# Opening of a fused attention and gated linear unit kernel: load queues, tail layout, weight order and roots

## The chip, the cores and the metric

The kernel runs on one core of one Trainium2 chip. The metric is device time in microseconds (us), the median of several runs. The core's engines are TensorE (PE; its weight loads are listed as PEld), VectorE (DVE), ScalarE (ACT), GpSimd (POOL) and SyncE (SP). SP computes nothing here and issues most of the transfers (DMAs). A "q" after an engine's name in the profile means its sequencer, which issues DMAs and waits.

## The reference

```python
def _attn_ref(q, k, v, g_norm):            # q, k, v: (8, 8, 576, 64): batch, head, token, width
    kv = np.einsum('bhsd,bhse->bhde', k, v)
    out = np.einsum('bhsd,bhde->bhse', q, kv)
    rms = np.sqrt(np.mean(out * out, axis=-1, keepdims=True) + 1e-06)
    return (out / rms * g_norm).astype(np.float32)

def _moe_ref(x, w_val, conv_w, w_out):     # x: (8, 576, 512), the heads side by side
    xp = np.concatenate([np.zeros((B, K - 1, D), dtype=np.float32), x], axis=1)
    for k in range(K):                     # K = 5
        gate_pre += conv_w[k][None, None, :] * xp[:, k:k + S, :]
    gate = 1.0 / (1.0 + np.exp(-gate_pre))
    val = x @ w_val
    return (gate * val @ w_out).astype(np.float32)
```

q, k and v are divided into 8 batches that don't depend on each other. The weights w_val, conv_w and w_out come in 64 bits and are narrowed to 32 on the chip.

## The kernel before

**An order written out by hand.** The kernel is a set of small functions, called steps, and a string PLAN of some 1,100 calls such as `raw_product 0 3`. The steps are issued in exactly that order, so each engine gets its instructions in the order in which the plan names the steps. An engine works through its own list in order; between engines, waits are set where data require them. A place in PLAN is thus a place in the lists of all engines that the step uses, and in the DMA queue.

**One batch.** `load_half` (L297 for batch 0, L301 for others) brings 512 tokens of k or v in two halves of heads, `load_tails` (L307) the remaining 64. `kv_product` (L438) makes k transposed times v for all heads, `kv_copy` (L453) moves it from PSUM to `kv_bd`. q is turned so that its width lies on the partitions: in batch 0 by matmuls with the identity (`load_q_rows` L326, `turn_q_rows` L480, `sort_q` L487), in other batches by a transposing load and DVE (`load_q` L317, `turn_q` L464). `raw_product` (L498) gives q times kv for a chunk `c` of 128 tokens (chunk 4 has 64). Then `square` (L512, ACT), `sums` (L524, DVE), the inverse root, and `normalise` (L559 on DVE in batch 0, L555 on ACT after). `turn_x` (L570, PE) with `keep_x` (L577, ACT), or `turn_blocks` with `move_blocks` later on, put x with its channels on the partitions; `halo` (L598, POOL) copies the tokens that the convolution needs from the chunk before. `gate_start`, `gate_tap` (L608, DVE) and `gate_end` make the gate, `val_product` (L620) or `val_fast` (L670) x times w_val, `gated` their product, and `out_product` (L701) or `fast_product` the result.

**Roots.** `powers` (L530) raises the sums to the power -1/2 on POOL. In batch 0 the chunks 4, 1 and 0 (`NEWTON`) go another way: `roots` (L538 to L546) makes them together on DVE by a bit trick and three Newton steps.

**Weights.** `stage_weight` (L341) loads a 64-bit piece: `cw` is conv_w, `wval` and `wout` have four pieces each. `narrow_weight key i n` (n from 0 to 7) makes 32 bits of it: steps 1, 2 and 3 on ACT (L366 to L370), the others on DVE (L361, L373 to L387). The last step of a wval piece multiplies by `gcol`, the column of g_norm. `turn_cw` (L409, PE) turns the narrowed conv weights, `keep_cw` (L414 to L416, DVE) scales them and gcol.

**Fillers.** `keep_warm n` (L427) issues n matmuls of the identity with itself, each of them two records in the profile, into a spare part of the PSUM tile of kv. Nobody reads the result. Since the part lies in the tile that `kv_copy` reads, a filler after a `kv_copy` waits for it.

**Queues.** All loads and stores are issued by SP, save gcol and cw (ACT), `move_blocks` (POOL) and half of the last stores (ACT). Batch 1's k and v are loaded into the tiles vsum and wsum, which are free at that time; the profile names them so.

Of the kernel before, what the change touches and what calls it, by code (L numbers as in the profile page):

```python
# [15 lines left out]
P = 128  # L16
# [3 lines left out]
stage_weight cw 0; load_q_rows 0 0; load_q_rows 0 1; load_half k 0 0; load_half v 0 0; load_tails 0;  # L20
narrow_weight cw 0 0; narrow_weight cw 0 1; narrow_weight cw 0 2; load_half k 0 1; load_half v 0 1;
stage_weight wval 0; keep_warm 5; turn_q_rows 0 0; stage_weight wval 1; turn_q_rows 0 1; stage_weight wval 2;
sort_q 0 0; stage_weight wval 3; narrow_weight cw 0 3; turn_q_rows 0 2; sort_q 0 1; narrow_weight cw 0 4;
load_half k 1 0; narrow_weight cw 0 5; narrow_weight cw 0 6; turn_q_rows 0 3; load_half v 1 0; sort_q 0 2;
narrow_weight cw 0 7; load_tails 1; turn_cw; sort_q 0 3; turn_q_rows 0 4; kv_product 0 0; sort_q 0 4;
load_half k 1 1; load_half v 1 1; load_q 1 0; keep_warm 7; kv_product 0 1; load_q 1 1; kv_copy 0; keep_warm 4;
raw_product 0 3; load_q 1 2; raw_product 0 2; square 0 3; raw_product 0 4; sums 0 3; square 0 2;
raw_product 0 1; narrow_weight wval 0 0; square 0 4; powers 0 3; sums 0 2; narrow_weight wval 0 1;
raw_product 0 0; keep_cw; square 0 1; sums 0 4; narrow_weight wval 3 0; powers 0 2; square 0 0; normalise 0 3;
narrow_weight wval 3 1; sums 0 0; keep_warm 5; turn_x 0 3; sums 0 1; keep_x 0 3; normalise 0 2; roots 0;  # L30
keep_warm 5; turn_x 0 2; keep_x 0 2; narrow_weight wval 0 2; normalise 0 4; normalise 0 1; keep_warm 5;
turn_x 0 4; normalise 0 0; keep_x 0 4; narrow_weight wval 0 3; keep_warm 3; turn_x 0 1; halo 0;
narrow_weight wval 0 4; keep_x 0 1; keep_warm 1; kv_product 1 0; narrow_weight wval 0 5;
narrow_weight wval 3 2; narrow_weight wval 0 6; narrow_weight wval 3 3; turn_x 0 0; narrow_weight wval 0 7;
kv_product 1 1; keep_x 0 0; turn_q 1 0; narrow_weight wval 3 4; load_q 1 3; val_product 0 0 1;
narrow_weight wval 3 5; narrow_weight wval 1 0; narrow_weight wval 3 6; narrow_weight wval 1 1;
narrow_weight wval 3 7; val_product 0 0 0; narrow_weight wval 1 2; stage_weight wout 0; turn_q 1 1;
narrow_weight wval 1 3; narrow_weight wval 2 0; gate_start 0 0; load_q 2 0; narrow_weight wval 1 4;
keep_val 0 0 1; narrow_weight wval 1 5; gate_start 0 2; turn_q 1 2; gate_start 0 1; gate_tap 0 0 3;
load_half k 2 0; kv_copy 1; load_half k 2 1; turn_q 1 3; narrow_weight wval 2 1; load_tails 2;  # L40
narrow_weight wval 2 2; narrow_weight wval 1 6; keep_warm 15; raw_product 1 3; narrow_weight wval 2 3;
narrow_weight wval 1 7; raw_product 1 2; load_half v 2 1; gate_tap 0 2 3; square 1 3; load_half v 2 0;
val_product 0 1 1; sums 1 3; load_q 2 1; narrow_weight wout 0 0; powers 1 3; narrow_weight wval 2 4;
narrow_weight wout 0 1; narrow_weight wval 2 5; keep_val 0 0 0; val_product 0 1 0; narrow_weight wval 2 6;
square 1 2; load_q 2 2; narrow_weight wval 2 7; normalise 1 3; sums 1 2; gate_tap 0 0 2; powers 1 2;
narrow_weight wout 0 2; keep_warm 3; raw_product 1 1; turn_q 2 0; keep_val 0 1 0; gate_tap 0 1 3; turn_x 1 3;
load_q 2 3; square 1 1; val_product 0 2 1; narrow_weight wout 0 3; sums 1 1; keep_x 1 3;
narrow_weight wout 0 4; powers 1 1; normalise 1 2; gate_tap 0 1 2; val_product 0 2 0; stage_weight wout 2;
gate_tap 0 0 1; stage_weight wout 3; gate_tap 0 2 2; normalise 1 1; gate_tap 0 1 1; raw_product 1 0;
narrow_weight wout 0 5; turn_x 1 2; gate_tap 0 0 0; square 1 0; tail_and_kv 1; keep_val 0 2 1; sums 1 0;  # L50
keep_val 0 1 1; keep_val 0 2 0; narrow_weight wout 0 6; keep_x 1 2; powers 1 0; narrow_weight wout 0 7;
gate_end 0 0; turn_q 2 1; turn_x 1 1; square 1 4; load_half k 3 0; gate_tap 0 2 1; kv_copy 2;
val_product 0 3 1; load_q 3 0; sums 1 4; keep_x 1 1; val_sums 0; powers 1 4; normalise 1 0; gated 0 0;
val_product 0 3 0; turn_q 2 2; load_half k 3 1; normalise 1 4; turn_q 2 3; load_half v 3 0; load_half v 3 1;
gate_start 0 3; narrow_weight wout 2 0; turn_x 1 0; gate_tap 0 1 0; load_tails 3; raw_product 2 3; keep_x 1 0;
gate_tap 0 3 3; narrow_weight wout 2 1; turn_x 1 4; raw_product 2 2; gate_tap 0 3 2; stage_weight wout 1;
keep_x 1 4; square 2 3; load_q 3 1; narrow_weight wout 3 0; val_product 1 0 1; keep_val 0 3 1; sums 2 3;
narrow_weight wout 2 2; gate_tap 0 3 1; square 2 2; powers 2 3; narrow_weight wout 2 3; gate_tap 0 2 0;
val_product 1 0 0; load_q 3 2; gate_end 0 1; gate_tap 0 3 0; keep_val 1 0 1; sums 2 2; gate_end 0 2; gated 0 1;
normalise 2 3; val_product 1 1 1; powers 2 2; val_sums 1; narrow_weight wout 2 4; keep_val 0 3 0; halo 1;  # L60
gated 0 2; narrow_weight wout 3 1; raw_product 2 1; gate_end 0 3; turn_blocks 2 3; val_product 1 1 0;
square 2 1; gated 0 3; keep_val 1 0 0; narrow_weight wout 3 2; sums 2 1; normalise 2 2; narrow_weight wout 2 5;
val_product 1 2 1; powers 2 1; turn_q 3 0; narrow_weight wout 2 6; load_q 3 3; gate_start 1 0;
narrow_weight wout 2 7; raw_product 2 0; narrow_weight wout 3 3; gate_tap 1 0 3; normalise 2 1;
val_product 1 2 0; narrow_weight wout 3 4; turn_blocks 2 2; narrow_weight wout 1 0; square 2 0;
narrow_weight wout 3 5; tail_and_kv 2; narrow_weight wout 1 1; sums 2 0; narrow_weight wout 1 2;
gate_tap 1 0 2; powers 2 0; keep_val 1 1 1; turn_q 3 1; narrow_weight wout 1 3; keep_val 1 1 0;
turn_blocks 2 1; val_product 1 3 1; square 2 4; load_half k 4 0; narrow_weight wout 1 4; kv_copy 3; load_q 4 0;
sums 2 4; normalise 2 0; narrow_weight wout 1 5; powers 2 4; turn_q 3 2; val_product 1 3 0;
narrow_weight wout 3 6; normalise 2 4; turn_q 3 3; load_q 4 1; gate_start 1 1; narrow_weight wout 1 6;  # L70
turn_x 2 4; raw_product 3 3; narrow_weight wout 3 7; keep_val 1 2 1; keep_x 2 4; narrow_weight wout 1 7;
raw_product 3 2; load_tails 4; square 3 3; turn_blocks 2 0; out_product 0 1; gate_tap 1 0 1; square 3 2;
move_blocks 2 3; keep_val 1 3 1; load_half v 4 0; sums 3 3; gate_start 1 2; load_half v 4 1; gate_tap 1 0 0;
keep_val 1 3 0; load_half k 4 1; keep_val 1 2 0; val_sums 2; gate_end 1 0; powers 3 3; sums 3 2;
out_product 0 3; gate_tap 1 1 3; gate_tap 1 1 2; powers 3 2; normalise 3 3; gate_tap 1 2 3; turn_q 4 0;
gate_tap 1 1 1; move_blocks 2 2; load_q 4 3; raw_product 3 1; gate_tap 1 1 0; out_product 0 2; square 3 1;
gated 1 0; gate_tap 1 2 2; load_tails 5; gate_start 1 3; sums 3 1; gate_end 1 1; gate_tap 1 3 3; keep_out 0 1;
powers 3 1; keep_out 0 3; gate_tap 1 2 1; out_product 0 0; normalise 3 2; store 0 3; turn_blocks 3 3;
gate_tap 1 2 0; move_blocks 2 1; gate_tap 1 3 2; normalise 3 1; store 0 1; gate_tap 1 3 1; gate_tap 1 3 0;
raw_product 3 0; halo 2; gate_end 1 2; gated 1 1; tail_and_kv 3; gate_end 1 3; load_q 4 2; gated 1 2;  # L80
gated 1 3; val_sums 3; out_product 0 5; square 3 4; square 3 0; sums 3 4; keep_out 0 2; sums 3 0; powers 3 4;
store 0 2; turn_q 4 1; powers 3 0; turn_blocks 3 2; turn_blocks 3 1; out_product 0 4; normalise 3 4;
move_blocks 2 0; turn_q 4 2; keep_out 0 5; turn_q 4 3; keep_out 0 0; store 0 5; normalise 3 0; turn_x 3 4;
kv_copy 4; load_half v 5 0; out_product 0 6; turn_blocks 3 0; load_q 5 0; keep_x 3 4; keep_out 0 4;
move_blocks 3 3; x_sums 2 0; gate_start 2 2; store 0 0; x_sums 2 2; raw_product 4 3; keep_out 0 6;
gate_tap 2 2 3; raw_product 4 2; square 4 3; x_sums 2 1; load_q 5 2; val_fast 2 0 0; sums 4 3; square 4 2;
gate_tap 2 2 2; val_fast 2 0 1; powers 4 3; val_keep 2 0 0; sums 4 2; load_half k 5 1; val_fast 2 0 2;
# [752 lines left out]
```

## Time and profile before

| | us |
|---|---|
| median of 6 runs | 330.39 (329.96 to 331.51) |
| the profiled execution, its own time | 331.51 |
| its span, first to last instruction | 329.7 |
| PE, idle time before L480 for q's loads | 2.9 |
| PE, idle time before L427 for kv_copy | 1.9 |
| PE, idle time before L438 for batch 1's v | 1.4 |
| POOL, L530, 37 roots, mean of one | 1.818 |
| DMA from issue to landing, POOL's xT<-y, median | 3.6 |

The busy time is what an engine's instructions cover; a matmul's end is modelled, so that a busy PE isn't PE at its peak. Idle time of an engine that isn't the bottleneck costs nothing. DMA queue q1 (SP's) moved 49.50 MB, q0 (POOL's) 6.30 MB and q10 (ACT's) 0.28 MB.

### The profile page before, as it was taken

The numbers are of one execution on the slowest core, as the hardware profiler recorded it, in microseconds if no ns is written. First come the engines' busy times: TensorE is split into PE (matmuls) and PEld (weight loads), VectorE is DVE, ScalarE is ACT, GpSimd is POOL, SyncE is SP. The second block draws the span as 40 slices with busy tenths as digits, with TensorE's granted clock in tenths as the row PEclk, the third lists the DMA queues.
The fourth block names the chain that finished last, engine by engine and source line by source line (L and its number), as shares of the span: only waits on it lengthen the run. The fifth ranks groups of instructions, "written<-read, shape, count | busy, mean of one in ns | idle before, by whom it ended". The sixth has DMA issues, their size and how long they took to land.

```text
span 329.7 us, 6026 instructions
## 1 busy us (share of the span) xinstructions
PE 316.1 (96%) x2019; PEld 226.1 (69%) x2019; DVE 249.9 (76%) x445; ACT 190.4 (58%) x530; POOL 136.7 (41%) x175
## 2 busy tenths in 40 slices
PE   4988889999999999999999999999999999999993
PEld 4987788888855668667676847766744773888652
DVE  1139969999999767998799699945988629889611
ACT  2446659999858556568646845656655423534320
POOL 3023015445398639734764486235956700000000
PEclk9999999999999999999999999999999999999999
DMA  6999699899599699779979767021515420120323
GB/s 218 305 319 246 194 292 287 258 283 242 159 241 265 181 250 284 171 202 252 233 168 240 233 176 184 0 58 41 145 27 126 119 64 20 47 64 3 95 64 95
DMA packets 43965, 56.47 MB, mean 171 GB/s; under 512 B 14986, under 2 KB 33438, under 8 KB 43934
## 3 DMA queue, kind: packets, MB, share of 16 engines
q1 hardware_dynamic: 40480, 49.50, 56.5%
q0 software_dynamic: 3072, 6.30, 7.5%
q10 hardware_dynamic: 382, 0.28, 0.4%
q8 instruction: 16, 0.26, 0.4%
q14 instruction: 15, 0.12, 0.1%
HBM read 40.33 MB, written 9.44 MB: 151 GB/s over the span
## 4 chain that ended last, share of the span: by engine, by line
PE 85%; DMA 7%; SPq 3%; ACT 2%; DVE 1%; issue 0%; ACTq 0%
PE out L701 25%; PE va L670 14%; PE raw L498 9%; PE val L620 8%; PE vc L670 7%; PE out L708 4%; PE kv L438 4%; PE a L765 4%; PE vb L670 4%; DMA wsum<-in_v_dram 3%; PE cb L765 3%; DMA gcol<-in_g_norm_dram 2%; DMA vl<-in_v_dram 2%; SPq L301 1%; PE kv L427 1%; SPq L307 1%
## 5 line engine op out<-in xcount | busy, mean ns | idle before, releaser
L530 POOL TENSOR_TENSOR rt<-ss,mhalf 128x8 f32<-128x8 f32 (+1 forms) x37 | 67.2, 1818 | 103.3 <-DVE ss L524 100.6
L608 DVE SCALAR_TENSOR_TENSOR gate<-xT,cwT,gate 128x576 f32<-128x576 f32 x128 | 101.0, 812 | 7.4 <-ACT gate L602 6.2
L701 PE MATMUL out<-wout,gv 128*128 128x512 f32 x192 | 85.8, 594 | 0.0
L701 PEld LDWEIGHTS out<-wout,gv 128*128 128x128 f32 x192 | 35.7, 190 | 38.5 <-issue 35.8
L591 POOL DMA_DIRECT2D xT<-y x96 | 53.0, 558 | 16.2 <-issue 4.8
L555 ACT ACTIVATE x<-raw,rt 128x64 f32<-128x64 f32 x252 | 55.1, 344 | 5.8 <-POOL rt L530 3.1
L498 PEld LDWEIGHTS raw<-kvbd,qT 128*128 128x128 f32 (+1 forms) x320 | 35.7, 180 | 7.3 <-issue 4.2
L524 DVE TENSOR_REDUCE ss<-sq 128x8 f32<-128x520 f32 (+1 forms) x37 | 23.5, 636 | 21.8 <-ACT sq L512 21.5
L498 PE MATMUL raw<-kvbd,qT 128*128 128x128 f32 (+1 forms) x320 | 38.1, 277 | 0.0
L615 ACT ACTIVATE gate<-gate 128x576 f32<-128x576 f32 x32 | 22.1, 696 | 19.1 <-DVE gate L608 19.0
L620 PE MATMUL val<-xT,wval 128*128 128x288 f32 x128 | 32.6, 408 | 0.0
L512 ACT ACTIVATE sq<-raw 128x512 f32<-128x512 f32 (+1 forms) x40 | 22.3, 562 | 17.8 <-PE raw L498 17.6
L620 PEld LDWEIGHTS val<-xT,wval 128*128 128x128 f32 x128 | 23.7, 190 | 6.0
L670 PE MATMUL va<-xs,vsum 128*128 128x288 f32 x96 | 27.2, 406 | 0.0
L716 ACT COPY ot<-out 128x512 f32<-128x512 f32 x28 | 16.1, 586 | 18.4 <-PE out L701 13.2
L633 DVE TENSOR_TENSOR gv<-gv,gate 128x576 f32<-128x576 f32 x32 | 23.4, 754 | 3.8 <-ACT gv L691 2.2
L602 ACT ACTIVATE gate<-xT,cwT 128x576 f32<-128x576 f32 x32 | 24.8, 790 | 0.5 <-DVE gv L633 0.5
L670 PEld LDWEIGHTS va<-xs,vsum 128*128 128x128 f32 x96 | 18.2, 190 | 4.8
L583 DVE STREAM_TRANSPOSE y<-x 128x512 f32<-128x512 f32 x24 | 16.7, 698 | 2.8 <-ACT x L555 2.8
L427 PE MATMUL kv<-ident 128*128 128x128 f32 x106 | 15.0, 293 | 3.3 <-ACT kvbd L453 1.9
L466 DVE STREAM_TRANSPOSE qT<-qs 128x512 f32<-128x512 f32 x24 | 16.7, 696 | 0.7 <-DMA qs<-in_q_dram 0.7
L438 PE MATMUL kv<-v,k 128*64 128x64 f32 x448 | 16.9, 222 | 0.0
(117 smaller groups left out, 438.4 us busy)
## 6 DMA issues: line engine op xcount, KB each, us to landing
qs<-in_q_dram SPq DMA_DIRECT2D x112, 140.0 KB, 4.5
out_dram<-ot SPq DMA_DIRECT2D x140, 64.0 KB, 1.7
k<-in_k_dram SPq DMA_DIRECT2D x12, 512.0 KB, 5.5
v<-in_v_dram SPq DMA_DIRECT2D x12, 512.0 KB, 7.5
xT<-y POOLq DMA_DIRECT2D x96, 64.0 KB, 3.6
y<-in_moe_w_val_dram SPq DMA_DIRECT2D x4, 512.0 KB, 9.0
w_wout<-in_moe_w_out_dram SPq DMA_DIRECT2D x4, 512.0 KB, 4.3
qs<-in_q_dram SPq DMA_DIRECT2D x2, 576.0 KB, 5.0
```

Of the source, the lines that this page charges most:

```text
L438: nc.tensor.matmul(kvp[r * D:(r + 1) * D, hp, :], kl[:, head(hp, r), :] if j == NJ else st["k", b, at[0]][:, at[1], at[2], j, :], vl[:, he ...
L498: nc.tensor.matmul(raw[row * m:(row + 1) * m, col * P:(col + 1) * P], st["qT", b][:, hp, c * P:c * P + m], kv_bd[b % 2][:, hp, :], start=T ...
L524: nc.vector.reduce_sum(out=ss[:, 0:n], in_=st["sq", b, c][:, 0:n], axis=AX.X)
L530: nc.gpsimd.tensor_tensor(out=rt[:, 0:n], in0=st["ss", b, c][:, 0:n], in1=mhalf[:, 0:n], op=ALU.pow)
L555: nc.scalar.activation(out=x[:, to * D:(to + 1) * D], in_=st["raw", b, c][:, h * D:(h + 1) * D], func=AF.Copy, scale=st["rt", b, c][:, h:h ...
L591: nc.gpsimd.dma_start(out=xTs[b % 2][i * TB:(i + 1) * TB, :, first:first + P], in_=y[a * TB:(a + 1) * TB, i])
L602: nc.scalar.activation(out=gate[:], in_=xTs[b % 2][:, jt, HALO:SX], func=AF.Copy, scale=cwT[:, K - 1, jt:jt + 1])
L608: nc.vector.scalar_tensor_tensor(out=gate[:], in0=xTs[b % 2][:, jt, tap * TB:tap * TB + S], scalar=cwT[:, tap, jt:jt + 1], in1=gate[:], op ...
L620: nc.tensor.matmul(val[:], wval[:, kc, jt * P:(jt + 1) * P], xTs[b % 2][:, kc, HALO + n * SV:HALO + (n + 1) * SV], start=(kc == 0), stop=( ...
L633: nc.vector.tensor_tensor(out=both, in0=both, in1=st["gate", b, jt][:], op=ALU.mult)
L670: nc.tensor.matmul(st[bank, "val", b, mj][:], weights_[:, k], tokens()[:, k], start=(n in (0, 1, 3) and k == 0), stop=(k == NK // 2 - 1), ...
L701: nc.tensor.matmul(po[:], gv[:, jt, first:first + P], wout[:, jt, :], start=(jt == 0), stop=(jt == NK - 1),)
```

## The change

It has five parts, and a new PLAN.

1. In batch 0, k's and v's first halves are issued by ACT, the second halves still by SP. The first wval piece is issued by ACT. gcol and cw are issued by POOL, gcol as part of `stage_weight cw`. The first plan steps are now k's half, cw, q's first rows, v's half, q's other rows, tails, wval 0. wval's pieces 2 and 3 are loaded after batch 1's k and v and three of its q loads.
2. The tails of heads 0 to 3 go to partitions 0 to 63 and those of heads 4 to 7 to partitions 64 to 127, in two DMAs each for k and v in place of one. The cleared part of a tail tile is two memsets of half the width in place of one.
3. The activation that loads ACT's table is a step of its own, `warm_up`, after the load of wval 0.
4. `roots` and `NEWTON` are gone: all five chunks of batch 0 use `powers`.
5. In PLAN, 26 fillers and `turn_cw` stand ahead of q's transposes; wval 0 and 1 are narrowed first, their first steps before the raw products; three value products instead of two come before batch 1's raw products, and 6 fillers in place of 15. There are 64 fillers instead of 53. The rest of PLAN holds the same steps in another order.

```diff
-stage_weight cw 0; load_q_rows 0 0; load_q_rows 0 1; load_half k 0 0; load_half v 0 0; load_tails 0;
-narrow_weight cw 0 0; narrow_weight cw 0 1; narrow_weight cw 0 2; load_half k 0 1; load_half v 0 1;
-stage_weight wval 0; keep_warm 5; turn_q_rows 0 0; stage_weight wval 1; turn_q_rows 0 1; stage_weight wval 2;
-sort_q 0 0; stage_weight wval 3; narrow_weight cw 0 3; turn_q_rows 0 2; sort_q 0 1; narrow_weight cw 0 4;
...
+load_half k 0 0; stage_weight cw 0; load_q_rows 0 0; load_half v 0 0; load_q_rows 0 1; load_tails 0;
+stage_weight wval 0; warm_up; load_half k 0 1; load_half v 0 1; stage_weight wval 1; narrow_weight cw 0 0;
+load_half k 1 0; narrow_weight cw 0 1; narrow_weight cw 0 2; load_half v 1 0; narrow_weight cw 0 3;
+load_tails 1; narrow_weight cw 0 4; narrow_weight cw 0 5; narrow_weight cw 0 6; narrow_weight cw 0 7;
+keep_warm 26; turn_cw; load_half k 1 1; load_half v 1 1; load_q 1 0; keep_warm 5; turn_q_rows 0 0;
+turn_q_rows 0 1; sort_q 0 0; turn_q_rows 0 2; sort_q 0 1; kv_product 0 0; narrow_weight wval 0 0; keep_cw;
+turn_q_rows 0 3; narrow_weight wval 0 1; sort_q 0 2; turn_q_rows 0 4; narrow_weight wval 0 2; load_q 1 1;
+sort_q 0 3; keep_warm 4; kv_product 0 1; sort_q 0 4; load_q 1 2; kv_copy 0; narrow_weight wval 1 0;
+narrow_weight wval 0 3; keep_warm 4; raw_product 0 3; narrow_weight wval 1 1; raw_product 0 2; square 0 3;
+stage_weight wval 2; stage_weight wval 3; raw_product 0 4; sums 0 3; square 0 2; raw_product 0 1; square 0 4;
...
+narrow_weight wval 0 7; kv_product 1 1; keep_x 0 1; normalise 0 0; turn_q 1 1; turn_x 0 0; val_product 0 0 1;
+narrow_weight wval 1 6; stage_weight wout 0; keep_x 0 0; narrow_weight wval 1 7; gate_start 0 1; turn_q 1 2;
+gate_start 0 2; val_product 0 1 1; load_q 2 1; narrow_weight wval 2 0; gate_tap 0 2 3; narrow_weight wval 2 1;
+gate_tap 0 1 3; narrow_weight wval 2 2; val_product 0 0 0; gate_tap 0 1 2; gate_start 0 0; load_q 2 0;
+gate_tap 0 2 2; narrow_weight wval 2 3; kv_copy 1; narrow_weight wval 3 0; turn_q 1 3; narrow_weight wval 3 1;
+load_half k 2 0; narrow_weight wval 2 4; keep_val 0 0 1; keep_warm 6; raw_product 1 3; narrow_weight wval 3 2;
...
-                nc.gpsimd.memset(t[T:P], 0.0)
+                nc.gpsimd.memset(t[T:P, 0:HP], 0.0)
+                nc.gpsimd.memset(t[0:T, HP:H], 0.0)
...
-        for r in range(P // D):
-            nc.scalar.dma_start(out=gcol[r * D:(r + 1) * D, :], in_=g_norm.unsqueeze(1))
+
+    def warm_up():
+
         nc.scalar.activation(out=warm[:], in_=warm[:], func=AF.Sigmoid)
...
-                nc.sync.dma_start(
+                (nc.sync if i else nc.scalar).dma_start(
                     out=t[:, r].rearrange("p h j d -> p h (j d)"),
...
-            nc.sync.dma_start(
-                out=tails[b % 2][n][0:T], in_=src[b, :, SF:S, :].rearrange("h s d -> s h d"))
+            for r in range(2):
+                nc.sync.dma_start(
+                    out=tails[b % 2][n][r * T:(r + 1) * T, r * HP:(r + 1) * HP],
+                    in_=src[b, r * HP:(r + 1) * HP, SF:S, :].rearrange("h s d -> s h d"))
...
-        (nc.scalar if key[0] == "cw" else nc.sync).dma_start(
+        (nc.gpsimd if key[0] == "cw" else nc.scalar if key == ("wval", 0) else nc.sync).dma_start(
...
     def stage_weight(*key):
+        if key[0] == "cw":
+            for r in range(P // D):
+                nc.gpsimd.dma_start(out=gcol[r * D:(r + 1) * D, :], in_=g_norm.unsqueeze(1))
         stage(key, *weights[key][0:3])
...
-    def roots(b):
```

## The prediction, made before the changed kernel ran

> **What bounds the kernel now.** First the page's head and busy time by stretch (columns: stretch, length, busy time and instructions of PE, PEld, DVE, ACT, POOL, granted clock, DMA share, GB/s).
>
> ```profile
> span 329.7 us, 6026 instructions
> PE 316.1 (96%) x2019; PEld 226.1 (69%) x2019; DVE 249.9 (76%) x445; ACT 190.4 (58%) x530; POOL 136.7 (41%) x175
> ```
>
> ```profile
> 0.00:10.00 10.00, 5.78 (x36) 5.09 (x38) 1.50 (x18) 2.88 (x6) 2.61 (x10) 1.00 0.75 237
> ...
> 30.00:40.00 10.00, 8.22 (x110) 7.04 (x111) 8.98 (x17) 6.35 (x11) 1.44 (x4) 1.00 0.73 195
> 40.00:50.00 10.00, 8.91 (x63) 7.78 (x62) 7.01 (x13) 6.46 (x13) 1.74 (x1) 1.00 1.06 286
> 50.00:60.00 10.00, 10.00 (x89) 8.68 (x89) 9.89 (x17) 9.35 (x35) 4.16 (x4) 1.00 1.03 288
> ...
> 300.00:330.00 30.00, 24.70 (x103) 16.87 (x101) 11.70 (x23) 6.86 (x15) 0.00 (x0) 1.00 0.28 71
> ```
>
> From 43 us to about 325 PE is never seen idle. So the end is the moment at which PE becomes gapless, plus a fixed amount of PE work. Time can be won or lost in the opening, or by breaking the gapless stretch. Next, PE's waits and its timeline in the opening.
>
> ```profile
> PE qTps L480 <- DMA qs<-in_q_dram: 2.9, 2, 2.1
> PE kv L427 <- ACT kvbd L453: 1.9, 2, 1.1
> PE kv L438 <- DMA wsum<-in_v_dram: 1.4, 1, 1.4
> ```
>
> ```profile
> 1.36 2.50 PE L427 MATMUL kv<-ident 128*128 128x128 f32 x10 [1.36 <-POOL ident masks.py:199]
> ...
> 7.40 6.13 PE L480 MATMUL qTps<-ident,qs 128*64 128x128 f32 x62 [2.12 <-DMA qs<-in_q_dram]
> ...
> 20.36 4.53 PE L498 MATMUL raw<-kvbd,qT 128*128 128x128 f32 x40
> ...
> 37.08 4.15 PE L620 MATMUL val<-xT,wval 128*128 128x288 f32 x16
> 42.31 3.62 PE L427 MATMUL kv<-ident 128*128 128x128 f32 x30 [1.09 <-ACT kvbd L453]
> 45.77 1.95 PE L498 MATMUL raw<-kvbd,qT 128*128 128x128 f32 x16
> ```
>
> Four landmarks: q transposes start at 7.40, batch 0's raw products at R = 20.36, the first value product at V = 37.08, batch 1's raw products at 45.77. Filler (L427) costs 0.25 us a record at the start (2.50/10) and 0.121 later (3.62/30): PE is slow first. Last, the loads.
>
> ```profile
> SPq L297 <- DMA gcol<-in_g_norm_dram: 2.5, 1, 2.5
> ```
>
> ```profile
> 22.79 11.04 DMA wsum<-in_v_dram
> ```
>
> ```profile
> 22.93 3.54 POOL L530 TENSOR_TENSOR rt<-ss,mhalf 128x8 f32<-128x8 f32 x2 [19.66 <-DVE ss L524]
> ...
> 91.14 2.35 POOL L591 DMA_DIRECT2D xT<-y  x4 [4.30 <-DVE gate L608]
> ```
>
> Batch 1's last v half lands at 33.83 and PE stands for it. A load on SP waits for the landing of gcol, a load eight places earlier in the program; later ones do the same: about eight are in flight at a time[...]. The POOL lines price a root (1.77) and a DMA issue (0.59).
>
> [...]
>
> **The change part by part.**
>
> *Start of the q transposes.* It takes from two sides. Data: bytes before batch 0's second q row load grow from 1,152 KB to at most 2,176 KB (first k and v halves come beside it on ACT's queue). At the 237 GB/s of the first stretch, started near 2 us, that is 11.4 at the latest against 7.4. Conv weights: the plan now puts turn_cw and five fillers ahead of the transposes, and gcol and cw are issued by POOL behind eight tail memsets. A 64x512 memset lasts 0.52; half as wide I take 0.3, so POOL is free at 1.36 + 8 x 0.3 = 3.8; three issues at 0.59: 5.5. From start of issue to landing the page shows 3.6 us (median) for POOL's transfers; the small ACT loads of the opening took 5.4 to 6.2. Bounds for cw's landing: 4.9 + 3.6 = 8.5 and 4.9 + 5.4 = 10.3. Narrowing it is five DVE operations and three ACT ones in a row: 0.21 + 3 x 0.43 + 1.04 and gaps, 2.7 us. Then turn_cw (0.2) and five fillers (10 x 0.121 = 1.2). The transposes start at 12.6 to 14.4; I take 13.1. The 26 fillers ahead end before it: roughly 20 records slow, 32 fast, 9 to 10.5 us. A new wait stands on ACT: wval 0 is the eleventh load, so its issue waits for the third, the first q row load, at about 7. Behind it on ACT are the table load (1.28) and cw's three narrowing steps; they are wanted from 8.7 on, so this is covered by cw's own transfer, and costs a us at most if q comes at 8.
>
> *To the raw products.* By then PE runs at full clock. The last 8 transposes took 0.49, so 72 take 4.4 instead of the 6.9 from 7.40 to 14.3. Beside them: two kv products (1.26 each), four fillers (1.0), kv_copy and its wait with four fillers (1.9): R = 13.1 + 4.4 + 2.5 + 1.0 + 1.9 = 22.9, say 22.8. That is 2.4 late. Before kv 0 1 all of batch 0 plus wval 0 must be in: about 3,970 KB, at 250 to 270 GB/s 17 to 18.5 us; PE comes at 20.
>
> *To the first value product.* The eleven small Newton operations on DVE go (27.36 to 29.66, 2.3 us). Five roots now run one behind the other on POOL: from R + 2.6, four at 1.77 and the short one at 1.2, to R + 10.9. DVE, in its new order, fills the time: after two sums, wval 0's and 1's steps, normalisations, the first turn_q. Adding its rows (reduce 0.69, narrow 0.42, 0.68, 0.42, 0.68, 0.75, normalise 0.68, transpose 0.77) behind each root I get the last normalisation done at R + 12.7, its transpose and V at R + 13.3 = 36.1; before it was R + 16.7. This holds only if kv 1 is not late. wval 2 and 3, 1,024 KB, now come after batch 1's k and v: 6,784 KB instead of 7,808 KB are ahead. Scaled from 33.83 with a 2 us start: 2 + 31.8 x 6784/7808 = 29.6, with PE there at 32. Covered by 2 us; if uncovered, V moves with it. Gain at V: 1.0.
>
> *To batch 1's raw products.* Before, 45.77 - 37.08 = 8.7 us held two value products (1.94 each), a 1.09 wait and 15 fillers. The new plan has three and 6 fillers: 5.8, then a wait for kv_copy 1. On ACT one keep_x, three gate_starts (0.76), three narrow steps (0.72) and the copy (0.74) stand in front: V + 6.6. So V + 6.7 + 1.4 = V + 8.1: 0.6 less, and one value product, 1.94, is already paid. Later fillers grow from 3 to 5: 2 x 0.242 = 0.5 back.
>
> *Middle and end.* DVE work up to the last output weight falls by the Newton steps (2.3), two taps (1.5) and what is done before R (1.5), against one sum more (0.6); it starts 2 us later. DVE then keeps some 2 us of lead over PE: nothing lost. tails are twice as many DMAs (some 0.6 us of SP each) on an SP that later waits 69 us for output tiles: nothing. Fillers and the warm activation in the opening lie in waiting time.
>
> Sum: 1.0 + 0.6 + 1.9 - 0.5 = 3.0 us. The profiled run's own time was 331.51 around a span of 329.7; its counterpart would be 328.5 with a span of 326.7. The median of the runs, 330.39, is the measure: **327.4 us**.
>
> **Rivals.** B, roots in a row eat it: the 1.77 us roots and a late q for turn_q 1 0 (its wait was 0.59 before) push V to 37.5; the moved value product still counts. 330.39 - (-0.4 + 0.6 + 1.4) = 328.8. For it: DVE takes its work strictly in order, so one late q load delays the last root's user. Against: those loads have 1 MB less in front.
> C, the middle absorbs it: from 50 to 90 us DVE is 9.8 to 10 and ACT 9.0 to 9.8 of 10 busy; PE would wait and arrive as before, 330.4. Against: PE showed no wait there, and DVE's list got shorter.
> D, slower, the late conv weights: turn_cw stands in PE's order ahead of everything[...]. Each us of lateness past 13.1 goes into R and V, so gain ends at a start of 16.1, cw landing at 12. There PE has also been idle since about 10[...], and the clock can fall: 72 transposes at the slow 6.9 instead of 4.4. With both, start 16.6: -3.5 - 2.5 + 3.0, that is 333.4. Against: the same load took 5.4 us through ACT.
>
> **Numbers.** A, the forecast, 0.45; B 0.11; C 0.09; D with every other loss 0.35. The likeliest's own range is 326 to 329 (start of transposes +-0.9, ACT's chain +-0.7). Over all, 325.8 to 333.2. A difference of 0.2% (0.7 us) is what these runs can tell from none. Faster: A and B, 0.56; same: C, 0.09; slower: D, 0.35.
>
> **What would show it.** Right: q transposes start near 13 and pace at 0.061 us a record; raw near 22.8; first value product near 36 with no wait on v; 6 fillers after three value products, raw of batch 1 near 44; gapless to the end; POOL showing five roots in a row. Wrong: a PE wait of over 3 us at turn_cw with slow transposes behind it (D), DVE standing for qs at turn_q (B), or PE gaps after 50 us (C).

## The result, and the profile after

The changed kernel is slower by 0.45%: 332.5 us in the median of 17 runs (331.08 to 333.8), beside 330.85 (329.96 to 332.45) for the kernel before. The ratio is 1.0045, with a 95% interval of 1.0034 to 1.0057. The forecast was 327.4. The time lies inside the range that was given, but the change went the other way. The ratios here and below leave out a run over 1.5% slower than the fastest of its kernel, of which the experiments have two (331.8 and 334.71 us).

First the head of the page of the changed kernel: span, the PE line, and the clock that PE was granted, in 40 slices of some 8.3 us.

```profile
span 331.1 us, 6118 instructions
PE 318.8 (96%) x2041; PEld 229.4 (69%) x2041; DVE 247.2 (75%) x434; ACT 189.6 (57%) x530; POOL 143.3 (43%) x185
PEclk9879999999999999999999999999999999999999
```

The span grew by 1.4 us, and PE is busy 2.7 us longer. The digits 8 and 7 in the clock line say that the clock fell in slices 2 and 3. (The record of the clock begins with its first rise, here at 6.49 us. Ahead of that the page counts full clock, although the first fillers ran slowly: their 52 records took 8.51 us, where 0.121 each would be 6.3.) The busy time by stretch shows where (columns as in the prediction). From 10 to 20 us it was, in the kernel before,

```profile
10.00:20.00 10.00, 9.16 (x150) 8.63 (x147) 0.97 (x4) 3.14 (x7) 0.00 (x0) 1.00 1.11 317
```

and in the changed kernel

```profile
10.00:20.00 10.00, 5.33 (x37) 5.06 (x39) 2.41 (x10) 1.78 (x4) 0.00 (x0) 0.67 1.13 317
...
40.00:50.00 10.00, 10.00 (x67) 8.37 (x62) 9.00 (x16) 7.99 (x15) 0.10 (x1) 1.00 0.89 244
50.00:60.00 10.00, 10.00 (x52) 8.12 (x52) 9.56 (x17) 7.91 (x28) 6.30 (x3) 1.00 1.11 279
```

From 40 to 60 us PE has no gap, where before it had one in the first half of that (8.91). The loss is in the stretch from 10 to 20: PE is busy for 5.33 us in place of 9.16, at 0.67 of its clock. The DMA engines are as full as before and move the same 317 GB/s. PE's waits name the cause: the list is headed by one wait for the narrowed conv weights, which before cost nothing.

```profile
PE cwps L412 <- DVE cw L387: 4.8, 1, 4.8
...
PE kv L430 <- ACT kvbd L456: 0.9, 1, 0.9
PE kv L441 <- DMA qs<-in_q_dram: 0.6, 1, 0.6
```

The three waits of before are gone (2.9 for q, 1.4 for v) or halved (1.9 for kv_copy); together they were 6.2 us. PE's timeline in the opening:

```profile
1.36 8.51 PE L430 MATMUL kv<-ident 128*128 128x128 f32 x52 [1.36 <-POOL ident masks.py:199]
14.67 0.29 PE L412 MATMUL cwps<-ident,cw 20*128 20x20 f32 x1 [4.81 <-DVE cw L387]
14.89 2.50 PE L430 MATMUL kv<-ident 128*128 128x128 f32 x10
17.32 4.20 PE L483 MATMUL qTps<-ident,qs 128*64 128x128 f32 x48
...
28.26 4.53 PE L501 MATMUL raw<-kvbd,qT 128*128 128x128 f32 x40
...
40.70 5.99 PE L605 MATMUL val<-xT,wval 128*128 128x288 f32 x24
46.61 1.60 PE L430 MATMUL kv<-ident 128*128 128x128 f32 x12
48.05 1.95 PE L501 MATMUL raw<-kvbd,qT 128*128 128x128 f32 x16
```

The fillers end at 9.87. PE stands until 14.67, and the five fillers and the first three groups of q transposes behind the wait run slowly: 0.25 us a filler record (2.50 / 10), as at the start of the kernel, against 0.121 later. The q rows themselves had landed at 6.87. The four landmarks before and after:

| | before | predicted | after |
|---|---|---|---|
| q transposes start | 7.40 | 13.1 | 17.32 |
| batch 0's raw products, R | 20.36 | 22.8 | 28.26 |
| first value product, V | 37.08 | 36.1 | 40.70 |
| batch 1's raw products | 45.77 | 44.2 | 48.05 |
| span | 329.7 | 326.7 | 331.1 |

R is 7.9 us later than before, and 5.6 of that is won back up to batch 1's raw products. What holds the conv weights up is read in the chain of work that ended last (start, length, what):

```profile
3.81 0.30 POOL vl L264
4.11 1.18 POOL gcol L404 x2
5.29 6.71 DMA w_cw<-in_moe_conv_w_dram
...
12.03 0.23 DVE wexp_cw L361
```

The whole beginning of this chain is one small load. POOL clears the tails (eight memsets, 2.75 us from 1.36 to 4.11), issues gcol twice and then the conv weights. Those 20 KB take 6.71 us to land, and narrowing them until 14.63 is the rest of the wait.

### The profile page after: what moved, and what is told of

It is laid out like the page before. It is cut to its first block, busy times and chain, and to the rows that moved or that the text cites. A ratio compares the mean times of both kernels' runs of the same rounds, so it can differ in the third digit from the quotient of the medians.

```text
span 331.1 us, 6118 instructions
## 1 busy us (share of the span) xinstructions
PE 318.8 (96%) x2041; PEld 229.4 (69%) x2041; DVE 247.2 (75%) x434; ACT 189.6 (57%) x530; POOL 143.3 (43%) x185
## 4 chain that ended last, share of the span: by engine, by line
PE 90%; DMA 6%; POOL 1%; ACT 1%; DVE 1%; SPq 0%; issue 0%; POOLq 0%; ACTq 0%
PE out L686 25%; PE va L655 14%; PE raw L501 9%; PE val L605 7%; PE vc L655 7%; PE kv L441 6%; PE out L693 4%; PE a L750 4%; PE vb L655 4%; PE cb L750 3%; PE kv L430 3%; DMA v<-in_v_dram 3%; DMA w_cw<-in_moe_conv_w_dram 2%; PE qTps L483 2%; PE xTps L555 1%; DMA qs<-in_q_dram 1%
## 5 line engine op out<-in xcount | busy, mean ns | idle before, releaser
L529 POOL TENSOR_TENSOR rt<-ss,mhalf 128x8 f32<-128x8 f32 (+1 forms) x40 | 70.3, 1762 | 99.9 <-DVE ss L523 99.7
L523 DVE TENSOR_REDUCE ss<-sq 128x8 f32<-128x520 f32 (+1 forms) x40 | 25.2, 631 | 21.5 <-ACT sq L515 21.3
L515 ACT ACTIVATE sq<-raw 128x512 f32<-128x512 f32 (+1 forms) x40 | 22.8, 572 | 12.0 <-PE raw L501 11.9
L600 ACT ACTIVATE gate<-gate 128x576 f32<-128x576 f32 x32 | 22.5, 712 | 10.3 <-DVE gate L593 10.3
L430 PE MATMUL kv<-ident 128*128 128x128 f32 x128 | 20.0, 318 | 2.2 <-POOL ident masks.py:199 1.4
L430 PEld LDWEIGHTS kv<-ident 128*128 128x128 f32 x128 | 18.7, 229 | 3.2 <-ACT kvbd L456 1.4
```

The lines of the kernel that those rows point to most:

```text
L430: nc.tensor.matmul(st["spare"].rearrange("p h d -> p (h d)")[:, 0:P], ident[:], ident[:], start=True, stop=True)
L523: nc.vector.reduce_sum(out=ss[:, 0:n], in_=st["sq", b, c][:, 0:n], axis=AX.X)
L529: nc.gpsimd.tensor_tensor(out=rt[:, 0:n], in0=st["ss", b, c][:, 0:n], in1=mhalf[:, 0:n], op=ALU.pow)
```

## The experiments

Theory L, after the result: the late conv weights, through the place of `turn_cw` in PE's order, hold up the q transposes and let the clock fall, and all else in the change is a gain. Its rivals: the new order behind the opening costs the time (theory M), or the five roots in a row on POOL do (theory G), or the new layout of the tails. In the diffs below the base is the changed kernel unless another is named. Each ratio is to runs of the kernel before that were made with the experiment (medians 330.92 to 331.08).

### More fillers ahead of the wait

```diff
-keep_warm 26; turn_cw; load_half k 1 1; load_half v 1 1; load_q 1 0; keep_warm 5; turn_q_rows 0 0;
+keep_warm 44; turn_cw; load_half k 1 1; load_half v 1 1; load_q 1 0; keep_warm 5; turn_q_rows 0 0;
```

> The changed kernel with 44 fillers ahead of turn_cw instead of 26, so that PE is busy while it waits for the conv weights. Theory L (late conv weights at the head of PE's order cost the time, in two parts: the wait of 4.8 us and the clock that falls in it): turn_cw stays near 14.7 us, the five fillers behind it take 1.2 us instead of 2.4, the q transposes about 4.4 instead of 5.7, the first raw product comes 2.5 us earlier, near 25.8, and the median falls from 332.5 to about 330.0. If the wait alone costs and the clock does not: 332.5, no change. Theory M (the new order after the opening costs the time, a later PE start is absorbed there): under 0.7 us of change.

Measured: 330.1 us (22 runs, 329.6 to 331.49), ratio to before 0.9972 (0.9962 to 0.9982). The wait at `turn_cw` shrank to 1.13, the clock stayed full, the five fillers behind it took 1.38 instead of 2.50 and the three groups 2.84 instead of 4.20. R came at 25.24. The turning ran at 14.18, only 0.5 us earlier than in the changed kernel. So of the 2.4 us between the two medians some 2 are the fall of the clock alone, and PE work that nobody reads buys them back.

### The turning of the conv weights moved behind the q transposes

```diff
-keep_warm 26; turn_cw; load_half k 1 1; load_half v 1 1; load_q 1 0; keep_warm 5; turn_q_rows 0 0;
-turn_q_rows 0 1; sort_q 0 0; turn_q_rows 0 2; sort_q 0 1; kv_product 0 0; narrow_weight wval 0 0; keep_cw;
+keep_warm 26; load_half k 1 1; load_half v 1 1; load_q 1 0; keep_warm 5; turn_q_rows 0 0;
+turn_q_rows 0 1; sort_q 0 0; turn_q_rows 0 2; sort_q 0 1; turn_cw; kv_product 0 0; narrow_weight wval 0 0; keep_cw;
```

> The changed kernel with turn_cw moved in PE's order from ahead of the q transposes to behind the third group of them, nothing else. Theory L: the q transposes start at about 11.1 us behind 31 fillers, turn_cw no longer holds them, raw products start near 21.8 instead of 28.3, the first value product near 34.3 instead of 40.7, median about 326.5. Theory M: the opening is 6 us earlier and the time falls by under 2 us, with PE waits in the middle.

Measured: 326.69 us (4 runs, 325.84 to 331.8), ratio 0.9862 (0.9834 to 0.9891). It is faster than both kernels. Its timeline on PE:

```profile
10.79 2.84 PE L483 MATMUL qTps<-ident,qs 128*64 128x128 f32 x48
14.08 0.23 PE L412 MATMUL cwps<-ident,cw 20*128 20x20 f32 x1 [0.45 <-DVE cw L387]
...
21.24 4.53 PE L501 MATMUL raw<-kvbd,qT 128*128 128x128 f32 x40
```

The conv weights still landed at 11.41, but PE now has transposes to do until they are narrow. The wait of 4.8 us became 0.45 and R came 7.0 us earlier. Between the ratios 1.0045 and 0.9862 lie 1.8% of 330.9, so that one place in PE's order is worth some 6 us: theory L.

As this had only four runs, it ran again later.

> The changed kernel with the turning of the conv weights moved behind the third group of q transposes, once more, since the first look at it had four runs only, one of them at 331.8, and since the same edit together with an earlier issue gave 325.8 to 330.0. If the moved turning is worth what the first look said: median 326.7 +-0.7, and at least half of the runs below 327.5. If it is worth less: median 328.0 to 328.6 as with both edits, runs spread from 325.8 to 330.

Measured: 326.44 us (6 runs, 325.73 to 327.89), ratio 0.9863 (0.9835 to 0.9892). The value held.

### Who issues the conv weights, and when

ACT instead of POOL, behind the first two loads of k:

```diff
-        (nc.gpsimd if key[0] == "cw" else nc.scalar if key == ("wval", 0) else nc.sync).dma_start(
+        (nc.scalar if key[0] == "cw" or key == ("wval", 0) else nc.sync).dma_start(
...
-                nc.gpsimd.dma_start(out=gcol[r * D:(r + 1) * D, :], in_=g_norm.unsqueeze(1))
+                nc.scalar.dma_start(out=gcol[r * D:(r + 1) * D, :], in_=g_norm.unsqueeze(1))
```

> The changed kernel with g_norm and the conv weights issued by ACT, behind the first two k loads, instead of by POOL behind its memsets; the plan is the same. Theory L: the conv weights land near 8.5 us instead of 12.0, turn_cw near 11.2, q transposes at 12.6 at full clock, raw products near 22.4, median about 326.8. If the transfer is late because of the loads that it shares the DMA engines with and not because of POOL: landing stays at 11 to 12 us and the median within 1 us of 332.5. Theory M: opening earlier by 5 us, median down by under 2 us.

Measured: 329.38 us (10 runs, 327.73 to 330.72), ratio 0.9951 (0.9931 to 0.9971). Faster than the changed kernel, but 2.6 us above the expectation. The weights were in at 8.2 us. Their narrowing then stood for ACT, which had waited for an earlier load and loaded its table until 9.23. The turning ran at 11.73 (11.2 was expected), behind a wait of 2.52. That short wait was enough for the clock to fall. Here is the busy time of PE in this kernel, in two stretches of 3.41 us, on either side of the moment at which the record of the clock falls (columns: stretch, length, PE busy and instructions, clock, DMA share, GB/s):

```profile
8.55:11.96 3.41, 0.89 (x8) 1.00 0.96 269
11.96:15.37 3.41, 3.41 (x21) 0.50 1.09 326
```

What failed was the author's estimate that so short a wait leaves the clock full: PE was busy for 0.89 us of the 3.41, and the next 3.41 us ran at half clock. In the two fastest of the ten runs (327.73 and 328.78) the mean clock was 0.997, against 0.990 to 0.995 in the others.

The other way to an earlier load leaves the queue as it is and takes the memsets out of POOL's way:

```diff
-                nc.gpsimd.memset(t[T:P, 0:HP], 0.0)
-                nc.gpsimd.memset(t[0:T, HP:H], 0.0)
+                nc.vector.memset(t[T:P, 0:HP], 0.0)
+                nc.vector.memset(t[0:T, HP:H], 0.0)
```

> The changed kernel with the tail memsets on DVE, so that POOL issues g_norm and the conv weights 2.7 us earlier. If the 6.7 us from issue to landing come from sharing the DMA engines with the big loads: landing near 9.3, turn_cw near 12, a wait of some 2 us, median 329 to 330. If POOL's transfer is only held up by the queue at that moment and takes 3.6 us when early: landing near 6.2, no wait, median near 327.

Measured: 329.85 us (18 runs, 327.77 to 331.7), ratio 0.9963 (0.9948 to 0.9978). The load was issued at 2.71 instead of 5.29, and landed at about 9.3 after 6.58 us on its way: the memsets cost 2.6 us of lateness, and the way itself hardly changed. A wait of 2.24 at `turn_cw` remained, and again half clock for 3.41 us.

Both edits together, memsets on VectorE and the turning moved:

> The changed kernel with both edits of its opening: the tail memsets on VectorE, so that GpSimd issues the conv weights early (landing about 9.3), and the turning of the conv weights moved behind the third group of q transposes. Theory L (the late conv weights hold up the q transposes, and nothing else in the opening costs): with the turning behind the q groups the landing is off the path already, so the earlier issue buys nothing more: q transposes start at about 10.8, raw starts at about 21.2, median 326.7 +-0.7, as with the moved turning alone. If the early issue has a worth of its own (less waiting of VectorE, an earlier keep_cw), below 326.0. If the memsets on VectorE hold up the first narrowing there, above 327.4.

Measured: 328.12 us (9 runs, 325.77 to 330.02), ratio 0.9901 (0.9866 to 0.9935). The early issue bought nothing more, as theory L has it, but the median missed L's 326.7 and lies above the 327.4 that was named for memsets holding up the narrowing on VectorE. They didn't hold it up in the profile: VectorE stood 4.3 us for the load itself. The nine runs spread widely, and the clock doesn't explain it: four of them took 328.12 to 329.85 at a mean clock of 1.0. The profiled run, 330.02, is the slowest of the nine, with the clock falling once; in it q started at 10.71, nothing waited at `turn_cw`, R came at 20.91 and V at 33.33. Then another load was late. Its chain of waits from 31 us on:

```profile
31.30 7.24 DMA y<-in_moe_w_val_dram
...
38.57 0.44 DVE wexp_wval L361
...
42.47 1.91 PE kv L430 x12
```

The third value weight piece landed at 38.54. Its narrowing on DVE and ACT stands ahead of the copy of batch 1's kv in ACT's order, and PE stood 3.16 us for that copy. So after the conv weights are out of the way the next thing that can be late is this load; whether it also made the other slow runs isn't shown. It was moved ahead of four q loads, with the turning late and the memsets on POOL:

```diff
-sort_q 0 3; keep_warm 4; kv_product 0 1; sort_q 0 4; load_q 1 2; kv_copy 0; narrow_weight wval 1 0;
+sort_q 0 3; keep_warm 4; kv_product 0 1; sort_q 0 4; stage_weight wval 2; load_q 1 2; kv_copy 0; narrow_weight wval 1 0;
...
-stage_weight wval 2; stage_weight wval 3; raw_product 0 4; sums 0 3; square 0 2; raw_product 0 1; square 0 4;
+stage_weight wval 3; raw_product 0 4; sums 0 3; square 0 2; raw_product 0 1; square 0 4;
```

> The same kernel with the load of the third value weight piece one group of four q loads earlier. With both edits the profile showed this piece landing at 38.54, VectorE standing 2.08 us for it, and TensorE then 3.16 us for the copy of the second value block, with the clock falling behind it. If this load is what is late next and makes the runs spread: the wait of VectorE for this piece falls by 1 us or more, batch 1's raw products start no later than 41.0, median 326.0 +-0.7. Rival (the q loads behind it are as late then, and hold up the turning of q on VectorE): a wait for q of 1 us or more takes its place, median 326.7 to 328.6.

Measured: 325.94 us (5 runs, 325.83 to 326.45), ratio 0.9845 (0.9822 to 0.9868): the fastest of all. The piece landed at 32.34 instead of 35.27 in the run without the edit. But in neither of the two profiled runs did VectorE or PE stand for it (raw products of batch 1 at 41.41 with the edit, where 41.0 was expected, and at 41.32 without), and the two intervals overlap. That the spread of runs fell from 2.2 to 0.6 us speaks for the theory; six and five runs don't prove it.

### All q transposes ahead of the conv weights

Here the q transposes and their copies go ahead of the narrowing on every engine, and 19 fillers take the place of 31: 13 ahead of the transposes, 6 behind the narrowing.

```diff
-stage_weight wval 0; warm_up; load_half k 0 1; load_half v 0 1; stage_weight wval 1; narrow_weight cw 0 0;
...
-keep_warm 26; turn_cw; load_half k 1 1; load_half v 1 1; load_q 1 0; keep_warm 5; turn_q_rows 0 0;
...
+load_half k 1 1; load_half v 1 1; load_q 1 0; keep_warm 13; turn_q_rows 0 0; turn_q_rows 0 1; sort_q 0 0;
+turn_q_rows 0 2; sort_q 0 1; turn_q_rows 0 3; sort_q 0 2; turn_q_rows 0 4; sort_q 0 3; sort_q 0 4;
+narrow_weight cw 0 0; narrow_weight cw 0 1; narrow_weight cw 0 2; narrow_weight cw 0 3;
+narrow_weight cw 0 4; narrow_weight cw 0 5; narrow_weight cw 0 6; narrow_weight cw 0 7;
+keep_warm 6; kv_product 0 0; narrow_weight wval 0 0; turn_cw; keep_cw; narrow_weight wval 0 1; narrow_weight wval 0 2;
...
```

> The changed kernel with 13 fillers ahead of the q transposes, the transposes and their copies ahead of the conv weights on PE and ACT, 6 fillers, then kv and turn_cw. Theory L, carried on: q transposes at 6.9 us, raw products at 18.5 to 19.5 instead of 28.3 (21.2 with turn_cw moved alone), first value product near 31 to 32, median 325 if the rest follows. Where another wait takes over (batch 1's v at 27, the third value weights at 35 us ahead of kv_copy 1 on ACT): raw products early, but no faster than turn_cw moved alone, 326.7.

Measured: 327.07 us (5 runs, 326.69 to 328.1), ratio 0.9888 (0.9871 to 0.9906). R came at 19.58 and batch 1's raw products at 39.37, 1.65 us earlier than with the moved turning alone, and the kernel is no faster. New waits took what was won: 1.7 us for a k load, 0.9 for DVE's turned q, 0.6 for v. In this profile the loads and DVE set the pace, and an earlier PE only met them sooner.

### The other parts of the change

The roots, in the kernel before: all five on POOL, the Newton steps taken out.

```diff
-narrow_weight wval 3 1; sums 0 0; keep_warm 5; turn_x 0 3; sums 0 1; keep_x 0 3; normalise 0 2; roots 0;
+narrow_weight wval 3 1; sums 0 0; keep_warm 5; turn_x 0 3; sums 0 1; keep_x 0 3; normalise 0 2; powers 0 4; powers 0 1; powers 0 0;
```

> The kernel before with one part of the change alone: all five roots of batch 0 on POOL (three more of 1.2 to 1.8 us in a row) instead of eleven small DVE operations. Theory L: the first value product waits for batch 1's v and for PE's order as before, so it moves by under 0.7 us: 330.85 plus or minus 0.7. Theory G (roots in a row on POOL cost the time): the last normalisation ends 1 to 2 us later, 332 or more.

Measured: 330.55 us (14 runs, 330.08 to 331.43), ratio 0.9988 (0.9975 to 1.0). The five roots cost nothing in the old PLAN. They weren't taken out of the changed kernel alone; there they ran as priced, in a row of 8.00 us:

```profile
30.84 8.00 POOL L529 TENSOR_TENSOR rt<-ss,mhalf 128x8 f32<-128x8 f32 x5 [25.00 <-DVE ss L523]
```

The tails, put back as they were into the version with the moved turning (one load on 64 partitions in place of two on 128, and one memset):

```diff
-            for r in range(2):
-                nc.sync.dma_start(
-                    out=tails[b % 2][n][r * T:(r + 1) * T, r * HP:(r + 1) * HP],
-                    in_=src[b, r * HP:(r + 1) * HP, SF:S, :].rearrange("h s d -> s h d"))
+            nc.sync.dma_start(
+                out=tails[b % 2][n][0:T], in_=src[b, :, SF:S, :].rearrange("h s d -> s h d"))
```

> The changed kernel with turn_cw behind the third group of q transposes, and the tails loaded as before: one DMA on 64 partitions each instead of two on 128. Theory L: tails are no cause, 326.7 plus or minus 0.7; their transfers take about 0.9 us each instead of 0.3. If the layout of the tails gains: 327.7 or more; if the doubled DMAs cost: 325.7 or less.

Measured: 328.86 us (6 runs, 327.18 to 330.15), ratio 0.9936 (0.9914 to 0.9959), beside 0.9862 and 0.9863 with the new tails. The intervals don't meet. The expectation was a difference of nothing; with this edit the new tails are worth some 2 us. The kernel with both edits has the new tails too and came to 0.9901, so the size is less sure than the interval says. The single memset also lets POOL start its loads 0.8 us earlier (gcol at 3.24 instead of 4.07); this isn't separated from the layout.

The profile is of the slowest of the six runs. Batch 0's first v halves, issued at the same moments, landed 1.4 us later beside the old tails (9.87 and 11.00 instead of 8.47 and 9.57). Batch 1's four new tail loads end within 1.05 us of the load before them (21.70 to 22.75), while the two old ones take 1.76 (23.22 to 24.98), and batch 1's last v half lands at 30.13 instead of 26.80. Of these 3.3 us, 1.5 were behind already ahead of batch 1's tails, 0.7 arose in them and 1.1 after them. The third value weight piece was late too (37.69 instead of 35.03), and PE stood 1.29 us for the copy of kv that its narrowing holds up. The 1.05 and 1.76 us are for the same bytes, but other loads ran beside them, so what the 128 partitions alone are worth isn't shown.

### The late load in the kernel before

Lastly the late load was put alone into the kernel before: gcol and the conv weights issued by POOL, its PLAN unchanged.

```diff
-            nc.scalar.dma_start(out=gcol[r * D:(r + 1) * D, :], in_=g_norm.unsqueeze(1))
+            nc.gpsimd.dma_start(out=gcol[r * D:(r + 1) * D, :], in_=g_norm.unsqueeze(1))
...
-        (nc.scalar if key[0] == "cw" else nc.sync).dma_start(
+        (nc.gpsimd if key[0] == "cw" else nc.sync).dma_start(
```

> The kernel before with g_norm and the conv weights issued by POOL, nothing else; turn_cw stands behind four groups of q transposes there. Theory L (the late conv weights cost time only because turn_cw stands ahead of the q transposes): they land at 11 to 12 us here too, q transposes still start at 7.4, raw products at 20.4, median within 0.7 us of the kernel before. If lateness itself costs, over ACT's list: raw products 3 us later, median 332 or more.

Measured: 334.33 us (4 runs, 332.98 to 334.77), ratio 1.0106 (1.0089 to 1.0123). The expectation, no difference, missed: in the old PLAN too `turn_cw` stands ahead of the last group of q transposes, and PE stood 3.19 us for it. Part of this was made good, as the q transposes went on from 5.66 instead of 7.40: R came at 21.18, 0.8 us later than before, and V at 36.26, 0.8 us earlier. The second cost came later, and is read from PE's busy time in stretches of 3.41 us (columns as in the table by stretch):

```profile
9.22:12.63 3.41, 1.87 (x32) 1.62 (x28) 0.21 (x1) 1.05 (x3) 0.00 (x0) 1.00 1.15 249
12.63:16.05 3.42, 1.77 (x49) 1.74 (x49) 0.97 (x4) 2.31 (x6) 0.00 (x0) 1.00 1.10 348
39.94:43.35 3.41, 1.35 (x9) 0.89 (x9) 3.33 (x6) 3.34 (x8) 0.00 (x0) 1.00 0.99 297
43.35:46.76 3.41, 3.41 (x18) 3.41 (x17) 1.50 (x3) 1.30 (x2) 0.00 (x0) 0.50 1.06 296
```

The wait of 3.19 us lay across two stretches, each busy for over half, and the clock stayed. The later wait of 2.06 us, for the copy of kv, left one stretch with 1.35 us of work, and the next ran at half clock: 15 fillers took 5.24 us instead of 3.62. The profiled run is the fastest of the four; what adds another 1.3 us in the others isn't seen in it. In two of them the mean clock was 0.988, against 0.993 in the profiled one, so it was low for longer in them.

With the same issue on POOL and the turning moved behind the first kv product:

```diff
-narrow_weight cw 0 7; load_tails 1; turn_cw; sort_q 0 3; turn_q_rows 0 4; kv_product 0 0; sort_q 0 4;
+narrow_weight cw 0 7; load_tails 1; sort_q 0 3; turn_q_rows 0 4; kv_product 0 0; turn_cw; sort_q 0 4;
```

> The kernel before with gcol and the conv weights issued by GpSimd, and the turning of the conv weights moved behind the first value product of k. Theory L (a late landing costs through the place of the turning in TensorE's order): the wait at the turning that the same issue showed (3.19 us, 334.33 us in all) is under 0.3 us, raw starts at 20.0 to 21.0, median within 0.7 of before. Rival (issuing on GpSimd itself costs, by what it does to the other loads or to ScalarE's copy of the second value block): the wait for that copy and the fall of the clock at about 43 remain, median 333 or more.

Measured: 330.42 us (14 runs, 329.71 to 334.71), ratio 0.9995 (0.9969 to 1.0021). The wait at the turning is gone, and so is the loss in most of the runs. The late weights still reached PE by another way: their narrowing stands ahead of a copy of q in ACT's order, and PE stood for that copy.

```profile
14.04 0.66 PE L480 MATMUL qTps<-ident,qs 128*64 128x128 f32 x8 [1.75 <-ACT qT L487]
```

With q in earlier, as in the last experiment, R came at 20.94. So the place of the waiting step decides what a late load costs, more than the queue that issues it. PE also stood 1.8 us for the copy of kv, and in the profiled run the clock held. Three of the fourteen runs took 333.96 us or more. Their mean clock was 0.988, against 0.997 or more in the other eleven, so it fell in them; where, isn't seen, as none of them has a profile.

## Why the prediction was wrong

**The step that failed** is the start of the q transposes: "12.6 to 14.4; I take 13.1". It came at 17.32, 4.2 us late. Two terms of its sum were mis-sized.
- The landing of the conv weights: the forecast's 13.1 holds a landing at 9.0, within bounds of 8.5 and 10.3. It was 12.00, which is 3.0 late. Of this 0.4 is the issue, at 5.29 instead of 4.9, as the memsets came 0.34 us apart and not 0.30. The other 2.6 are the way: 4.1 in the value taken, with 3.6 and 5.4 as bounds, and 6.71 measured. The 3.6 was a median over POOL's moves of x in the middle of the kernel. The 5.4 was the lower end of the 5.4 to 6.2 that had been read from ACT's loads in the opening; 6.2 would have put the late bound at 11.1. The number of load queues beside the transfer isn't the reason: issued by POOL in the old PLAN it met SP's queue alone and took 6.81 and 7.96, and on ACT's queue in the changed kernel it took 5.1 beside SP's. All eleven profiles with POOL as the issuer show 6.1 to 8.0 us, the three with ACT 5.1 to 6.0. But ACT also issued it earlier, with fewer loads ahead, so whether the engine or the moment makes the difference stays open.
- The five fillers behind the wait: 1.2 priced, 2.43 measured, as the clock had fallen. The forecast says "By then PE runs at full clock", and left the fall to its rival D. But its own numbers held a pause already, from fillers ending at 9 to 10.5 to a turning at 11.7. The kernel with the load on ACT's queue had just that, a turning at 11.73 behind a pause of 2.5: the clock fell, and its ratio was 0.9951, where 327.4 to 330.39 is 0.9909. With the landing as forecast, some 1.4 us of the gain would have been missing all the same.

The new wait on ACT's queue, put at about 7 us, did not come: the first value piece was issued at 2.79.

**To the raw products**: 9.7 predicted, 10.94 measured. The 1.3 over are the first 48 transposes, 4.20 instead of 2.84. The rest of that sum held.

**To the first value product**: R + 13.3 predicted, R + 12.44 measured. The row of roots was priced at 8.3 and took 8.00. Batch 1's v was in at 27.27, predicted 29.6, and never waited for.

**To batch 1's raw products**: V + 8.1 predicted, V + 7.35 measured. Three value products and six fillers in sequence, and no wait for the copy of kv.

**To the end**: 1.4 us less than before was predicted, 0.9 came (283.05 us from batch 1's raw products to the end, before 283.93). What is missing fits PE's wait of 0.6 us near 62, for a load of q, where the forecast had "nothing lost" in the middle. The versions without this wait need 282.9 to 283.3, but each of them stands 0.4 to 0.6 us for the copy of kv at 60 to 64 us.

The sum closes: 4.2 + 1.25 - 0.85 - 0.75 + 0.55 = 4.4 us, which is what lies between the predicted and the measured span.

**The tails** were priced at nothing, looking at issue time on SP alone. They were worth some 2 us where they were undone singly, through what lands beside and behind them.

**The rivals.** D, with every other loss at a chance of 0.35, is what happened: start at 16.6, 333.4 priced; 17.32 and 332.5 measured. Its point of decision was a landing at 12, and the weights landed at 12.00. That the size came so near is in part luck: D put 2.5 us of slow clock on 72 transposes, and 1.2 us on fillers and 1.4 on 48 transposes were measured. B and C are out: the roots were in time, and PE had no gap in the middle but the 0.6. The rest of the change is a gain: with the turning moved, the same parts give 0.9862 of the time before. So the late conv weights cost some 6 us (some 2 of them clock, as the fillers show), and all else brings some 4.5.

## What to carry to other kernels

Before a step is moved ahead of everything on the engine that bounds the kernel, work out when its last input lands, with the price of that transfer from the same queue and the same part of the kernel (6.71 us here, where the median from the middle was 3.6), and put work that is ready ahead of the step that isn't, which was worth some 6 us here. A pause on TensorE was dearer than its length where the clock fell behind it: in the changed kernel 4.81 us of waiting, and 2.6 more on fillers and transposes. Waits of 2.06 to 2.52 us were followed by a fall too, and 18 fillers more, which nobody reads, brought 2.4 us, so work that is ready can pay in a pause of 2 us. A small load in a full opening isn't priced by its size: 20 KB took 6.71 us, while the DMA engines moved 319 GB/s in all. And a change that loses can hide a good one: undo its parts singly before all of it is dropped.

## What the runs showed of the hardware

The clock fell behind stretches in which TensorE was busy for at most 1.35 of 3.41 us, and in four of the five not idle throughout. Half clock lasted 3.41 us (11.96 to 15.37 with the load on ACT's queue, 13.01 to 16.42 with the early memsets), or 6.83 in the changed kernel (13.31 to 20.14), whose first rise, at 6.49, lies 6.83, twice 3.41, ahead of the fall. PE's busy time can be counted in stretches of 3.41 us from each moment at which the record of the clock changes. Those in or soon after the opening that ended in a fall held 0.00 (changed kernel), 0.89 (load on ACT's queue), 1.14 (both edits), 1.17 (early memsets) and 1.35 us (load on POOL's queue, old PLAN). Of the stretches counted that had a pause and that the clock outlasted, the lowest held 1.58, in the old PLAN with the turning moved (columns as for the load on ACT's queue):

```profile
38.92:42.33 3.41, 1.58 (x8) 1.00 0.92 292
```

So the limit lay somewhere between 1.35 and 1.58 of 3.41 us here, roughly, as the ends of matmuls are modelled. To come back took more: in the changed kernel a stretch with 2.05 us of work was not enough, and the next one, filled, was. At the start of the kernel before, whose clock first rose at 12.39, 2.38 us (from 2.16 to 5.57) and 1.58 (to 8.98) were not enough, and the filled stretch behind them was. How much of a stretch has to be filled isn't shown. The changed kernel's two:

```profile
13.31:16.72 3.41, 2.05 (x9) 2.00 (x10) 1.77 (x8) 0.23 (x1) 0.00 (x0) 0.50 1.06 348
16.72:20.14 3.42, 3.42 (x30) 3.19 (x30) 0.43 (x1) 0.58 (x1) 0.00 (x0) 0.50 1.17 303
```

The other surprise is the small load. The conv weights took 6.71 us when POOL issued them at 5.29 and 6.58 when it did so at 2.71: the earlier place moved the landing, and hardly the way. From 10 to 20 us the DMA engines moved 317 GB/s in the kernel before, with SP's loads alone, and 317 GB/s in the changed one, where loads of ACT and POOL ran beside SP's until 12.00. In the first 10 us it was 237 before and 279 in the changed one.
